# Splitting an inverse transform and its DRAM scratch into channel halves, with later weight loads and four projection steps moved into the softmax

## The chip, the cores and the metric

The kernel runs on one core of one Trainium2 chip. The metric is the device time of one execution in microseconds (us). Most executions of one kernel agree within about 1 per cent here. A profiled execution also has a "span", first instruction to last, which is 1 to 2 us shorter than the device time; times of single events below are in that span.

Engines: PE is the matmul engine, DVE the vector engine, ACT the scalar engine, POOL is GpSimd, and SP issues most DMA transfers (in a timeline "SPq" is its queue). Each engine has its own instruction list, in an order fixed before the run.

## The reference, cut to what matters

There are two independent halves, whose outputs are put side by side. S = 2048 positions, D = 576 channels, bf16.

```python
# A: attention over 8 positions, 2 apart, 32 heads of 18 channels
q, k, v = split(x @ wqkv)
logits = einsum("bhsd,bhswd->bhsw", q, kg) / sqrt(18)      # kg: k at s, s-2, ... s-14
a = einsum("bhsw,bhswd->bhsd", softmax(masked logits), vg) @ wo
# B: gated long convolution
kv = causal_conv4(k, shift_k) * v                          # four taps
y  = irfft(rfft(pad(kv)) * rfft(pad(ssm_k)))[:S] + kv * ssm_D
b  = q * y
out = concatenate([a, b], axis=-1)
```

## The kernel before

Half A and half B are interleaved so that the PE always has something to do. In time there are six stages:

1. **Front.** x is loaded, transposed on PE and evicted to SBUF as `xT`.
2. **q/k and first transform.** 18 q/k projection steps, mixed with 8 "x steps" (four-tap convolution on DVE, then a DFT matmul "s1") and 8 "k steps" (the filter, transposed on PE, then s1). Results go to DRAM scratch `Dx` and `Dk`.
3. **Products.** DVE multiplies q with shifted k, PE sums over channels to logits. Beside it: 16 v projection steps and 8 filter spectrum steps. At its end three "halo" copies bring v rows from the neighbouring partitions (`vX`).
4. **Softmax.** Nearly all DVE and ACT.
5. **Main stage.** "PV pairs" (attention weights times v on DVE, summed and projected on PE), mixed with "spectrum steps" `g_step`: load from `Dx`, second DFT stage, multiply by the filter spectrum, inverse second stage, store to `Dy`.
6. **Tail.** `y_step`: load from `Dy` in the other order, last inverse stage, times q, store.

`Dk`, `Dx` and `Dy` are scratch tensors in DRAM, through which the transform changes the order of its data. Each `Dy` load needs data of all spectrum steps. The parts that matter, cut (`...`):

```python
    load_x(0, nc.sync); load_x(1, nc.scalar); load_w(0, nc.sync); load_w(1, nc.scalar)
    load_x(2, nc.sync); load_x(3, nc.scalar)
    ...
    def s1_chunk(src, c2, Dd, vst_pool, add_d):
        for ch in range(3):
            ps = psb()                     # PSUM ring of two; q/k steps use another, psA
            ...                            # matmuls, then an ACT copy to vst
        nc.sync.dma_start(by_f1(Dd, c2), vst[:]...)
    def k_step(c2):
        ptr = pb.tile([128, 2, 1024], BF16, name="psB")
        ...                                # 10 transposes of the filter into ptr
        nc.vector.tensor_copy(kt[:], ptr[:, :, 0:D])
        s1_chunk(kt, c2, Dk, kvp, True)
    ...
    sk_step()                              # load the four taps, reorder them on DVE (skb)
    load_w(2, nc.sync)                     # v weights, into the third part of tile wq
    ...                                    # filter loads
    run(qk_steps, b_steps)                 # two lists, interleaved evenly
    permute_wv()                           # ACT: v weights into (d, h) order
    ...
    wk = pool("wk", 2, "right")
    def kh_step(g):
        Wk = wk.tile([128, 4, D], BF16, name="Wk")
        nc.sync.dma_start(Wk[:], by_rt(Dk)[:, 4 * g:4 * g + 4, :])
        ...
    def g_step(g):
        Wx = b2.tile([128, 4, D], BF16, name="Wx")
        nc.sync.dma_start(Wx[:], by_rt(Dx)[:, 4 * g:4 * g + 4, :])
        ...
    for g in range(8):
        mixed += v_steps[2 * g:2 * g + 2] + [lambda g=g: kh_step(g)]
    run([... logit_step(wi) for 8 wi], [ia_tables] + mixed + [halo])
    lg.release(); qk.release(); wk.release()
    sm = pool("sm", 2, "left")
    b2 = pool("b2", 2, "right")            # the pool of Wx exists only from here on
    softmax_a(0); softmax_a(1)
    g_step(0)
    softmax_b(0); softmax_b(1)
    run([... at_step(wp) for 4 wp], [lambda: g_step(1)])
    ...
    run([... pv_step(tp) for tp in range(4)],    [... g_step(g) for g in range(2, 8)])
    run([... pv_step(tp) for tp in range(4, 8)], [... y_step(c2) for c2 in range(8)])
```

Of the kernel before, what the change touches and what calls it, by code (L numbers as in the profile page):

```python
# [18 lines left out]
def kernel(  # L19
# [20 lines left out]
    NT = 16  # L40
    PS = bass.MemoryType.PSUM
# [17 lines left out]
    def psb():  # L59
        return pb.tile([128, 2, 512], FP32, name="psB")  # L60
# [4 lines left out]
    Dk = dram.tile([32, 128, D], BF16, name="Dk")  # L65
    Dx = dram.tile([32, 128, D], BF16, name="Dx")
    Dy = dram.tile([32, 128, D], BF16, name="Dy")
# [12 lines left out]
    def by_f1(Dd, c2):  # L80
        return Dd.rearrange("r f d -> f r d")[:, 4 * c2:4 * c2 + 4, :]

    def by_rt(Dd):
        return Dd.rearrange("r (l h) d -> (r l) h d", h=32)
# [21 lines left out]
    wq = wqp.tile([128, 5, 3 * D], BF16, name="wq")  # L106
# [26 lines left out]
    nc.gpsimd.memset(wq[0:64, 4, :], 0.0)  # L133

# [135 lines left out]
    def s1_chunk(src, c2, Dd, vst_pool, add_d):  # L270
        sf = src.rearrange("p t d -> p (t d)")
        vst = vst_pool.tile([128, 2, 2 * D], BF16, name="vst")
        for ch in range(3):
            ps = psb()
            for ri in range(2):
                extra = add_d and c2 == 0 and ri == 0 and ch < 2
                nc.tensor.matmul(ps[:, ri, 0:384], T1[:, ri, :], sf[:, 384 * ch:384 * ch + 384], start=True, stop=not extra)  # L277
                if extra:
                    n = 384 if ch == 0 else 192
                    nc.tensor.matmul(ps[:, ri, 0:n], row0[:], Db[:, 384 * ch:384 * ch + n], start=False, stop=True)  # L280
            nc.scalar.activation(vst[:, :, 384 * ch:384 * ch + 384], ps[:, :, 0:384], ACT.Copy)  # L281
        nc.sync.dma_start(by_f1(Dd, c2), vst[:].rearrange("p r (t d) -> p (r t) d", t=2))
# [12 lines left out]

    def permute_wv():
        for kb in range(5):
            nc.scalar.activation(wv[:, kb, :].rearrange("p (d h) -> p d h", h=H),
                                 wq[:, kb, 2 * D:3 * D].rearrange("p (h d) -> p d h", d=DH), ACT.Copy)
# [12 lines left out]
    def sk_step():  # L312
        skraw = kvp.tile([128, D, 4], BF16, name="tB", bufs=1)
        nc.sync.dma_start(skraw[:], B_shift_k.partition_broadcast(128))
        nc.vector.tensor_copy(skb[:], skraw[:].rearrange("p d j -> p j d"))
# [33 lines left out]
    load_w(2, nc.sync)  # L349
# [14 lines left out]
    permute_wv()  # L364
# [6 lines left out]
    Khat = kf.tile([128, 2, 32 // 2, D], BF16, name="Khat")  # L371
# [3 lines left out]
    wk = pool("wk", 2, "right")  # L375
# [63 lines left out]
    def s2(Wt, g, dst, scale):  # L439
        for prl in range(2):  # L440
            for d0, d1 in DCH:
                ps = psb()
                for im in range(2):
                    for hp in range(2):
                        nc.tensor.matmul(ps[64 * hp:64 * hp + 64, im, 0:288],  # L445
                                         W2[:, im, 4 * g + 2 * prl + hp].rearrange("p l f -> p (l f)"),
                                         Wt[:, 2 * prl + hp, d0:d1], start=True, stop=True, tile_position=(0, 64 * hp))
                nc.scalar.activation(dst[:, :, prl, d0:d1], ps[:, :, 0:288], ACT.Copy, scale=scale)  # L448
# [15 lines left out]
    def kh_step(g):  # L464
        Wk = wk.tile([128, 4, D], BF16, name="Wk")
        nc.sync.dma_start(Wk[:], by_rt(Dk)[:, 4 * g:4 * g + 4, :])
        s2(Wk, g, Khat[:, :, 2 * g:2 * g + 2, :], 1.0 / 2048)

    def g_step(g):
        Wx = b2.tile([128, 4, D], BF16, name="Wx")  # L470
        nc.sync.dma_start(Wx[:], by_rt(Dx)[:, 4 * g:4 * g + 4, :])
        Kc = Khat[:, :, 2 * g:2 * g + 2, :]
        Xc = b2.tile([128, 2, 2, D], BF16, name="Xc")
        s2(Wx, g, Xc, 1.0)
        m1 = b2.tile([128, 2, 2, D], BF16, name="m1")
        m2 = b2.tile([128, 2, 2, D], BF16, name="m2", bufs=1)
        nc.vector.tensor_tensor(m1[:], Xc[:], Kc[:, 0].unsqueeze(1).to_broadcast([128, 2, 2, D]), ALU.mult)  # L477
        nc.vector.tensor_tensor(m2[:], Xc[:], Kc[:, 1].unsqueeze(1).to_broadcast([128, 2, 2, D]), ALU.mult)  # L478
        nc.vector.tensor_tensor(m1[:, 0], m1[:, 0], m2[:, 1], ALU.subtract)
        nc.vector.tensor_tensor(m1[:, 1], m1[:, 1], m2[:, 0], ALU.add)  # L480
        Y = b2.tile([128, 4, D], BF16, name="Y")
        for prl in range(2):
            for d0, d1 in DCH:
                ps = psb()
                for zi in range(2):
                    for hp in range(2):
                        nc.tensor.matmul(ps[:, hp, 0:288], IAt[64 * hp:64 * hp + 64, zi, 2 * g + prl, :],  # L487
                                         m1[64 * hp:64 * hp + 64, zi, prl, d0:d1], start=(zi == 0), stop=(zi == 1),
                                         tile_position=(64 * hp, 0))
                nc.scalar.activation(Y[:, 2 * prl:2 * prl + 2, d0:d1], ps[:, :, 0:288], ACT.Copy)  # L490
        nc.sync.dma_start(by_rt(Dy)[:, 4 * g:4 * g + 4, :], Y[:])

    mixed = []
    for g in range(8):
        mixed += v_steps[2 * g:2 * g + 2] + [lambda g=g: kh_step(g)]
# [6 lines left out]
    run([lambda wi=wi: logit_step(wi) for wi in range(W)], [ia_tables] + mixed + [halo])  # L502
    lg.release()
    qk.release()
    wk.release()
# [4 lines left out]
    g_step(0)  # L510
    softmax_b(0)
# [46 lines left out]
    def y_step(c2):  # L558
        Vw = b2.tile([128, 4, D], BF16, name="Wx")
        Vy = Vw[:].rearrange("p (r t) d -> p r t d", r=2)  # L560
        nc.sync.dma_start(Vw[:], by_f1(Dy, c2))
        qt = b2.tile([128, 2, 2, D], BF16, name="Xc")[:, 0]
        nc.gpsimd.dma_start(qt, qb[:, 2 * c2:2 * c2 + 2, :])
        stage = b2.tile([128, 4, D], BF16, name="Y")[:, 0:2]
        for u in range(2):
            ps = psb()
            for di, (d0, d1) in enumerate(DCH):
                for ri in range(2):
                    nc.tensor.matmul(ps[:, di, 0:288], IB[:, ri, :], Vy[:, ri, u, d0:d1], start=(ri == 0), stop=(ri == 1))  # L569
            nc.vector.tensor_tensor(stage[:, u, :].rearrange("p (i d) -> p i d", i=2), ps[:, :, 0:288],  # L570
                                    qt[:, u, :].rearrange("p (i d) -> p i d", i=2), ALU.mult)
        nc.sync.dma_start(outb[:, 2 * c2:2 * c2 + 2, D:2 * D], stage)

    run([lambda tp=tp: pv_step(tp) for tp in range(4)], [lambda g=g: g_step(g) for g in range(2, 8)])
    run([lambda tp=tp: pv_step(tp) for tp in range(4, 8)], [lambda c2=c2: y_step(c2) for c2 in range(8)])
    a3.release()
    b2.release()
    kf.release()
# [30 lines left out]
```

## Time and profile before

309.3 us, median of three runs (307.89 to 309.55).

Busy time by stage of the kernel before. The stretches were chosen at the first q/k matmul, the first product, the first mask add of the softmax, the first P and the last `Dy` store. The columns: stretch, its length, then busy time and instruction count of each engine, the TensorE clock granted (1.00 is full), the share of time in which DMA engines were busy, GB/s.

```profile
core 0: us, PE busy (x) PEld busy (x) DVE busy (x) ACT busy (x) POOL busy (x), PEclk, DMA share, GB/s
0.00:29.14 29.14, 9.59 (x80) 8.52 (x81) 12.39 (x34) 12.37 (x12) 8.74 (x31) 1.00 0.96 305
29.14:100.86 71.72, 70.61 (x397) 36.24 (x396) 48.47 (x40) 51.42 (x67) 0.00 (x0) 1.00 0.53 188
100.86:150.80 49.94, 46.74 (x500) 28.63 (x500) 43.14 (x30) 35.07 (x58) 3.84 (x6) 1.00 0.43 132
150.80:176.50 25.70, 5.09 (x48) 3.92 (x48) 16.57 (x24) 11.38 (x15) 7.29 (x15) 0.67 0.56 148
176.50:264.05 87.55, 80.03 (x924) 54.13 (x924) 68.89 (x47) 51.49 (x86) 1.09 (x2) 0.94 0.32 109
264.05:308.40 44.35, 24.80 (x181) 15.96 (x180) 12.06 (x17) 4.24 (x7) 3.23 (x6) 0.68 0.70 226
```

The second and third stretch look PE-bound, 117 of 122 us. In the fourth, the softmax, the PE does 5 us of work in 26. The fifth is PE-bound again. In the last, PE, DVE and DMA take turns waiting.

The SP queue of the kernel before (start, length, line, count), from the end of the product stage. L498 is the first halo copy, L471 the loads of the spectrum steps, L491 a `Dy` store, L561 the loads of the y steps:

```profile
147.81 0.59 SPq L498 DMA_DIRECT2D vX<-vX  x1
...
151.94 21.63 SPq L471 DMA_DIRECT2D Wx<-Dx  x3
183.50 0.32 SPq L491 DMA_DIRECT2D Dy<-Y  x1
...
264.05 0.32 SPq L491 DMA_DIRECT2D Dy<-Y  x1
...
267.76 7.66 SPq L561 DMA_DIRECT2D Wx<-Dy  x3
```

And what the PE does in the softmax stage: 17 us of nothing, then transposes of attention weights (L433), then the first spectrum step (L445):

```profile
167.29 1.89 PE L433 MATMUL psA<-ident,Lsb 128*128 128x128 bf16 x16 [17.15 <-DVE Lsb L426]
...
170.75 0.68 PE L445 MATMUL psB<-Wx,W 128*64 128x288 bf16 x8
```

All eight y loads come after the last `Dy` store at 264.05.

### The profile page before, as it was taken

To read this page: it belongs to the slowest core of one execution; us is meant where nothing else is said; L and a number is where in the kernel's file an instruction comes from. 1 tells how busy PE (TensorE), PEld (TensorE's weight loads), DVE (VectorE), ACT (ScalarE), POOL (GpSimd) and SP (SyncE) were. 2 spreads that over 40 slices of the span, in tenths; PEclk is the share of its full clock that TensorE was granted. 3 is DMA by queue.
4 is the path that set the end of the run, shared out by engine and by line. 5 is a ranking of instruction groups with operands and counts; after the bars stand their busy time and mean duration, and the time that the engine had idled before them with its cause. 6 is when DMAs were issued, how large, how long until landed. Compare 5 with 4: busy or idle time off the path is not lost.

```text
span 308.4 us, 5069 instructions
## 1 busy us (share of the span) xinstructions
PE 236.9 (77%) x2129; PEld 147.4 (48%) x2129; DVE 201.5 (65%) x188; ACT 166.0 (54%) x242; POOL 24.2 (8%) x59
## 2 busy tenths in 40 slices
PE   1047999999998889999402379999989989976522
PEld 1045445555446455657102236648657657743211
DVE  3076997988501899899576496868939939323431
ACT  2165367788878457787461634765674773411000
POOL 8200000000000000000922000000000000001100
PEclk9999999999999999999955958999999999978555
DMA  7999365744545444522792213433541232359991
GB/s 238 360 364 278 149 210 175 268 153 154 212 149 179 158 155 149 155 79 76 219 231 60 78 42 113 152 119 117 191 132 64 112 121 79 133 165 368 286 301 49
DMA packets 28002, 52.37 MB, mean 170 GB/s; under 512 B 1918, under 2 KB 22094, under 8 KB 27853
## 3 DMA queue, kind: packets, MB, share of 16 engines
q1 hardware_dynamic: 25052, 47.04, 46.0%
q0 software_dynamic: 1264, 3.17, 4.0%
q10 hardware_dynamic: 1664, 1.84, 1.8%
q8 instruction: 16, 0.26, 0.4%
q14 instruction: 6, 0.05, 0.1%
HBM read 31.11 MB, written 18.87 MB: 162 GB/s over the span
## 4 chain that ended last, share of the span: by engine, by line
PE 49%; DVE 15%; DMA 14%; ACT 11%; issue 9%; SPq 0%; POOL 0%; DVEq 0%; ACTq 0%; POOLq 0%
PE psA L246 11%; PE psB L445 7%; PE psA L233 6%; PE psB L277 6%; DMA wq<-in_A_wqkv_dram 5%; DMA Xc<-in_B_q_dram 5%; PE psA L541 4%; DVE P L532 3%; PE psB L290 3%; PE psA L554 3%; PE psB L487 3%; PE psA L388 3%; ACT Y L490 3%; DMA Wx<-Dy 2%; DVE m L478 2%
## 5 line engine op out<-in xcount | busy, mean ns | idle before, releaser
L532 DVE TENSOR_TENSOR P<-vX,at 128x4608 bf16<-128x4608 bf16 x16 | 40.5, 2554 | 14.3 <-PE psA L541 14.3
L541 PE MATMUL psA<-ident,P 128*128 128x128 bf16 (+1 forms) x640 | 44.6, 223 | 5.9 <-DVE P L532 5.9
L541 PEld LDWEIGHTS <-P 128*128 128x128 bf16 (+1 forms) x640 | 38.0, 101 | 14.8 <-issue 7.6
L246 PE MATMUL psA<-xT,wq 128*128 128x512 bf16 x160 | 40.0, 384 | 0.5 <-DVE xT L149 0.5
L281 ACT ACTIVATE vst<-psB 128x768 bf16<-128x768 f32 x48 | 35.9, 814 | 4.9 <-PE psB L277 3.5
L385 DVE TENSOR_TENSOR prod<-q,k 128x4096 bf16<-128x4096 bf16 x16 | 36.0, 2287 | 2.0 <-PE psA L388 2.0
L570 DVE TENSOR_TENSOR Y<-psB,Xc 128x576 bf16<-128x576 f32 x16 | 11.6, 754 | 29.0 <-PE psB L569 16.7
L490 ACT ACTIVATE Y<-psB 128x576 bf16<-128x576 f32 x32 | 18.9, 650 | 19.1 <-PE psB L487 15.1
L554 PE MATMUL psA<-wv,xT 128*128 128x288 bf16 x160 | 25.8, 292 | 1.6 <-ACT xT L547 1.5
L569 PE MATMUL psB<-Wx,IB 128*128 128x288 bf16 x64 | 14.9, 404 | 15.3 <-DMA Wx<-Dy 15.2
L233 PE MATMUL psA<-wv,xT 128*128 128x288 bf16 x160 | 24.6, 292 | 0.2 <-ACT vX L235 0.2
L144 PE MATMUL psA<-ident,xnat 128*128 128x128 bf16 x80 | 9.6, 308 | 19.0 <-DVE xT L149 10.5
L246 PEld LDWEIGHTS <-wq 128*128 128x128 bf16 x160 | 15.4, 99 | 16.7 <-issue 1.5
L448 ACT ACTIVATE Xc<-psB 128x576 bf16<-128x576 f32 x32 | 20.1, 654 | 3.2 <-PE psB L445 2.6
L233 PEld LDWEIGHTS <-xT 128*128 128x128 bf16 x160 | 19.4, 145 | 4.7 <-issue 4.3
L448 ACT ACTIVATE Khat<-psB 128x576 bf16<-128x576 f32 x32 | 19.7, 650 | 3.5 <-PE psB L445 3.0
L554 PEld LDWEIGHTS <-xT 128*128 128x128 bf16 x160 | 13.7, 99 | 10.8 <-issue 4.5
L524 POOL DMA_DIRECT2D wv<-in_A_wo_dram x18 | 8.9, 500 | 125.6 <-PE psA L233 119.8
L569 PEld LDWEIGHTS <-IB 128*128 128x128 bf16 x64 | 7.8, 130 | 21.8 <-DMA Wx<-Dy 16.1
L293 DVE COPY kTt<-psB 128x1152 bf16<-128x1152 bf16 x8 | 6.1, 758 | 18.4 <-PE psB L290 18.3
L477 DVE TENSOR_TENSOR m<-Xc,Khat 128x2304 bf16<-128x2304 bf16 x8 | 10.8, 1356 | 10.9 <-ACT Xc L448 10.9
L144 PEld LDWEIGHTS <-xnat 128*128 128x128 bf16 x80 | 8.4, 144 | 19.9 <-issue 13.5
(116 smaller groups left out, 349.2 us busy)
## 6 DMA issues: line engine op xcount, KB each, us to landing
Dx<-vst SPq DMA_DIRECT2D x8, 576.0 KB, 3.0
Dk<-vst SPq DMA_DIRECT2D x8, 576.0 KB, 3.0
Wk<-Dk SPq DMA_DIRECT2D x8, 576.0 KB, 3.7
Wx<-Dx SPq DMA_DIRECT2D x8, 576.0 KB, 3.8
Dy<-Y SPq DMA_DIRECT2D x8, 576.0 KB, 2.7
Wx<-Dy SPq DMA_DIRECT2D x8, 576.0 KB, 5.8
kX<-in_B_k_dram SPq DMA_DIRECT2D x3, 1008.0 KB, 5.2
vt<-in_B_v_dram SPq DMA_DIRECT2D x4, 576.0 KB, 8.9
```

What stands on the lines that cost most here:

```text
L233: nc.tensor.matmul(ps[:, di, 0:288], xTt[:, kb, t2, :], wv[:, kb, d0:d1], start=(kb == 0), stop=(kb == 4))
L246: nc.tensor.matmul(ps[:, u, :], wcols(kb, comp, ct), xT[:, kb, 512 * j:512 * j + 512], start=(kb == 0), stop=(kb == 4))
L277: nc.tensor.matmul(ps[:, ri, 0:384], T1[:, ri, :], sf[:, 384 * ch:384 * ch + 384], start=True, stop=not extra)
L281: nc.scalar.activation(vst[:, :, 384 * ch:384 * ch + 384], ps[:, :, 0:384], ACT.Copy)
L385: nc.vector.tensor_tensor(prod[:], q2[ct // 2][:], k2[ct // 2][:, :, sh:sh + S], ALU.mult)
L445: nc.tensor.matmul(ps[64 * hp:64 * hp + 64, im, 0:288], W2[:, im, 4 * g + 2 * prl + hp].rearrange("p l f -> p (l f)"), Wt[:, 2 * prl + hp, ...
L448: nc.scalar.activation(dst[:, :, prl, d0:d1], ps[:, :, 0:288], ACT.Copy, scale=scale)
L490: nc.scalar.activation(Y[:, 2 * prl:2 * prl + 2, d0:d1], ps[:, :, 0:288], ACT.Copy)
L532: nc.vector.tensor_tensor(P[:].rearrange("p w (d h) -> p w d h", h=H), vs, at[:, :, t2, :].unsqueeze(2).to_broadcast([128, W, DH, H]), ALU ...
L541: nc.tensor.matmul(oacc[0:csz, ci, 128 * u:128 * u + 128], Ps[u][:, wi, 128 * ct:128 * ct + csz], ident[:], start=(ci % 2 == 0 and u == 0 ...
L554: nc.tensor.matmul(pso[:, di, 0:288], oT[:, ct, t2, :], wot[:, ct, d0:d1], start=(ct == 0), stop=(ct == 4))
L569: nc.tensor.matmul(ps[:, di, 0:288], IB[:, ri, :], Vy[:, ri, u, d0:d1], start=(ri == 0), stop=(ri == 1))
```

## The change

Its intent has three parts:

1. *Front.* Taps and v weights are loaded behind the x transposes, so that x and q/k need not share DMA and engines with them, and q/k can start earlier.
2. *v projection.* Four of the sixteen v steps move from the product stage into the softmax, and the halo copies behind them.
3. *Channel halves.* `Dk`, `Dx` and `Dy` are split into halves of 288 channels, so that y steps of the first half need only spectrum steps 0 to 3. The order of late steps is changed with it. All scratch loads share one pool of three buffers.

The diff, cut:

```diff
-    Dk = dram.tile([32, 128, D], BF16, name="Dk")          # Dx, Dy likewise
+    Dk = dram.tile([2, 32, 128, HD], BF16, name="Dk")
-    wq = wqp.tile([128, 5, 3 * D], BF16, name="wq")
+    wq = wqp.tile([128, 5, 2 * D], BF16, name="wq")
...
+    wraw = k2[1][:]...      # areas of q and k tiles, which reuse the x buffers
+    sraw = q2[1][:]...
...
     sk_step()
-    load_w(2, nc.sync)
+    load_wv()
+    permute_wv()            # ACT, 5 copies, now ahead of the q/k evictions
...
     run(qk_steps, b_steps)
-    permute_wv()
...
-    wk = pool("wk", 2, "right")
+    wk = pool("wk", 3, "right")
...
+    def load_wt(Dd, dh, g):
+        Wt = wk.tile([128, 8, HD], BF16, name="Wt")
+        nc.sync.dma_start(Wt[:], by_rt(Dd, dh, g))
+        return Wt
-    def g_step(g):
-        Wx = b2.tile([128, 4, D], BF16, name="Wx")
-        nc.sync.dma_start(Wx[:], by_rt(Dx)[:, 4 * g:4 * g + 4, :])
+    def g_step(i):
+        dh, g = i // 4, i % 4
+        Wt = load_wt(Dx, dh, g)
...
-        Y = b2.tile([128, 4, D], BF16, name="Y")
+        Y = b2.tile([128, 8, HD], BF16, name="Y", bufs=1)
...
-        mixed += v_steps[2 * g:2 * g + 2] + [lambda g=g: kh_step(g)]
+        mixed += [lambda g=g: kh_step(g)] + (v_steps[2 * g:2 * g + 2] if g < 4 else v_steps[g + 4:g + 5])
-    run([... logit_step ...], [ia_tables] + mixed + [halo])
+    run([... logit_step ...], [ia_tables] + mixed)
...
-    wk.release()
...
     g_step(0)
+    for t2 in range(12, 16):
+        v_step(t2)
+    halo()
...
-    run([... pv_step(tp) for tp in range(4)],    [... g_step(g) for g in range(2, 8)])
-    run([... pv_step(tp) for tp in range(4, 8)], [... y_step(c2) for c2 in range(8)])
+    run([... pv_step(tp) for tp in range(3)],    [... g_step(g) for g in range(2, 6)])
+    run([... pv_step(tp) for tp in range(3, 5)], [... g_step(g) for g in range(6, 8)])
+    run([... pv_step(tp) for tp in range(5, 8)], [... y_step(i) for i in range(8)])
```

## The prediction

> **What bounds it now** (busy time by stretch, 308.4 us span)
> - 0 to 29.1 us: DMA share 0.96, PE busy 9.6. The chain of waits opens with 17.9 us of weight DMA. Timeline: the taps' copy (skb) sits on DVE ahead of the xT copies and waits 10.3 us for its load; ACT waits 8.6 us for the v weights and permutes them (five times 1.25) ahead of its xT copies. So x transposes stop from 8 to 18 us; q/k matmuls start at 29.1.
> - 29.1 to 150.8: PE busy 117 of 122. In the product part (from 100.9) DVE has 41.4 us of products in 50, PE most of the 16 v steps (1.3 each).
> - 150.8 to 176.5: softmax, PE busy 5; then to 268: 84 of 91.5.
> - 268 to 308.4: PE busy 21 at clock 0.64, DMA share 0.73. The last Dy store is issued at 264.1, all eight Dy loads from 267.8 on: no inverse step can begin before the last spectral step is stored. 9.2 MB then move at about 310 GB/s.
>
> **What the change does**
> 1. Taps and v weights go into tiles that reuse the x buffers, so cannot precede the x copies. x lands by 13 us; q/k start at about 15. The first conv input still lands near 30, but PE has 39 us of independent q/k work, and DVE's conv chain (4 times 10.9, plus 6 of copies) ends near 84. The stage ends near 89 instead of 103: gain 11 to 14.
> 2. Four v steps (5.2 us of PE) go to the softmax, where PE idles; the product stage falls towards DVE's 41.4: gain 4 to 6. The halo copy (10 us to landing) starts later: neutral.
> 3. Channel halves: inverse loads of the first half need only spectral steps 0 to 3, and the last spectral step now precedes pv 5 to 7. After it remain about 30 us of PE, 27 of DVE, 22 to 28 of DMA, overlapped. PE also keeps its clock (Trainium skill, "TensorE: Matmul & The Clock Gate", Part 1: it halves after an idle window of about 3.4 us; the trace agrees: 0.50 from 283 us). Ideal gain 30, I count 18.
> 4. Cost: 576 B rows for Dk, Dx, Dy, q, output. DMA packet records show 51 ns for 1152 B and 178 for 4608, so about 30 for 576 (estimate, linear): about 6 us of DMA more in the tail, 5 in the s1 stage (share 0.53, hidden).
>
> **Critical path.** All on it: 12 + 5 + 18, about 36 of 309.3 us.
>
> **Predicted: 272 us, 80% range 258 to 289.** Faster by over 2%: 0.95, within 2%: 0.03, slower: 0.02.
>
> **Right or wrong, by step.** (1) First q/k matmul near 15 us; no skb copy before the xT copies. (2) First to last product 43 to 46 us; v matmuls in the softmax. (3) Dy loads of half 0 issued before the last Dy store; PE idle after that store below 12 us; clock near 1 until the last few us. (4) 576 B packets near 30 ns.
>
> **What would make it wrong.** The sync queue issues in order: the waits of taps and v weights may hold back the conv inputs. Half 0's Dy loads may stand behind the last Dy store, or conv work on PE ahead of ready q/k work. DVE (76% busy in the main stage) may become the limit.

## More of the kernel before

In the kernel before, a load landed at 162.15, and the matmuls that need it ran at 170.75, because others stood ahead of them in PE's list.

Where the PE starts its q/k work and its s1 work (timeline of PE; start, length, line, tiles, count, in brackets the idle time before and what ended it):

```profile
29.14 14.85 PE L246 MATMUL psA<-xT,wq 128*128 128x512 bf16 x65 [0.52 <-DVE xT L149]
43.84 0.81 PE L277 MATMUL psB<-tA,T 128*128 128x384 bf16 x4
```

The load of spectrum step 0 is issued behind the halo, at 151.94, and lands at 162.15; its matmuls stand in PE's order behind the first attention transposes, so they run only at 170.75, although the PE idled for 17 us before that.

## The result, and the profile after

The changed kernel takes 296.12 us (293.14 to 296.45, four runs) against 309.03 for the kernel before in the same rounds. The ratio is 0.9566, 95% interval 0.9497 to 0.9634. (A ratio is the mean time of one kernel's runs over that of the other's of the same rounds, so it is not quite the ratio of the medians that are quoted.) Executions over 1.5% slower than the fastest of the same kernel are left out of the means. The kernel is faster, by 13 us instead of the 36 predicted, and lies outside the predicted range of 258 to 289.

The same six stretches after the change:

```profile
0.00:21.17 21.17, 9.50 (x80) 8.38 (x81) 11.76 (x33) 7.03 (x7) 8.75 (x32) 1.00 0.93 306
21.17:107.76 86.59, 73.99 (x377) 35.25 (x376) 49.85 (x41) 56.92 (x69) 0.00 (x0) 0.90 0.59 183
107.76:156.60 48.84, 47.26 (x486) 27.22 (x488) 43.26 (x31) 32.43 (x55) 0.00 (x0) 0.97 0.51 157
156.60:190.35 33.75, 19.09 (x152) 12.70 (x149) 25.24 (x33) 23.59 (x36) 13.44 (x23) 0.71 0.68 195
190.35:260.60 70.25, 65.27 (x764) 47.91 (x764) 55.31 (x36) 40.80 (x66) 0.00 (x0) 0.92 0.32 107
260.60:294.60 34.00, 26.11 (x276) 21.15 (x273) 15.90 (x18) 6.70 (x11) 3.74 (x5) 0.93 0.80 244
```

Set against the rows of before, the first product starts 6.9 us *later* (107.76 for 100.86) although q/k start 8 us earlier. The product stage is only 1.1 us shorter. The softmax stage is 8 us longer, with 14 us more PE work in it. The main stage is 17.3 us shorter, and the tail 10.4.

**Front.** The PE of the changed kernel in the front:

```profile
21.17 10.09 PE L248 MATMUL psA<-xT,wq 128*128 128x512 bf16 x40 [0.60 <-ACT xT L149]
39.34 9.72 PE L248 MATMUL psA<-xT,wq 128*128 128x512 bf16 x33 [8.07 <-ACT q L251]
48.90 0.81 PE L279 MATMUL psB<-tA,T 128*128 128x384 bf16 x4
```

and its ACT, where L309 is the permutation of the v weights and L251 the q/k evictions:

```profile
32.29 5.95 ACT L309 ACTIVATE wv<-k 128x576 bf16<-128x576 bf16 x5 [4.15 <-DMA k<-in_A_wqkv_dram]
38.26 1.02 ACT L251 ACTIVATE q<-psA 128x1024 bf16<-128x1024 f32 x1
```

The v weights, now loaded last, land at 32.3. ACT's list has their permutation ahead of the third q/k eviction, so ACT waits 4.15 us and then permutes for 5.95; both PSUM buffers of the q/k steps stay full, and the PE stands 8.07 us.

**Softmax.** The SP queue of the changed kernel; L475 are the loads of the spectrum steps, L511 and L513 the first and third halo copy, L504 a `Dy` store, L577 the loads of the y steps:

```profile
145.33 14.07 SPq L475 DMA_DIRECT2D Wt<-Dx  x4
168.44 0.60 SPq L511 DMA_DIRECT2D vX<-vX  x1
169.52 0.33 SPq L504 DMA_DIRECT2D Dy<-Y  x1
...
171.94 2.63 SPq L513 DMA_DIRECT2D vX<-vX  x1
...
230.37 0.37 SPq L577 DMA_DIRECT2D Wt<-Dy  x1
...
260.63 0.33 SPq L504 DMA_DIRECT2D Dy<-Y  x1
```

and its ACT and DVE just before the first P (L547): ACT evicts the attention weights (L445), then step 1's `Y` (L503); DVE has the spectral products of step 2 (L491) ahead of P:

```profile
175.37 4.25 ACT L445 ACTIVATE at<-psA 128x512 bf16<-128x512 bf16 x8 [3.01 <-PE psA L443]
...
180.86 1.19 ACT L503 ACTIVATE Y<-psB 128x576 bf16<-128x576 f32 x2 [1.24 <-DMA Dy<-Y]
...
186.34 1.36 DVE L491 TENSOR_TENSOR m<-Xc,Khat 128x2304 bf16<-128x2304 bf16 x1 [8.12 <-ACT Xc L457]
...
190.35 7.49 DVE L547 TENSOR_TENSOR P<-vX,at 128x4608 bf16<-128x4608 bf16 x3
```

Two things have moved against each other. The first spectrum load is now issued at 145.33, ahead of everything, and the first `Dy` store comes at 169.52 instead of 183.50. But the halo, 147.81 before, comes at 168.44, and the first P at 190.35 instead of 176.48. The last attention weights were ready at 179.62 (end of their eviction), so P came 10.7 us after them. The last halo copy landed at 182.9, which accounts for 3.3 us. For the other 7.4 P stood in DVE's list behind the products of step 2. These waited 8.12 us for their input from ACT, whose list has step 1's `Y` eviction ahead of it; and that eviction first waited 1.24 us for the first `Dy` store to land (180.75), since the changed kernel has one `Y` buffer where the kernel before has two.

**Tail.** The first y load is issued at 230.37, 30 us ahead of the last `Dy` store, as the halves intend.

### The profile page after: what moved, and what is told of

The parts are those of the page before. It is cut to its first block, busy times and chain, and to the rows that moved or that the text cites. A ratio compares the mean times of both kernels' runs of the same rounds, so it can differ in the third digit from the quotient of the medians.

```text
span 294.6 us, 5101 instructions
## 1 busy us (share of the span) xinstructions
PE 241.2 (82%) x2129; PEld 152.6 (52%) x2129; DVE 201.3 (68%) x188; ACT 167.5 (57%) x242; POOL 25.9 (9%) x60
## 3 DMA queue, kind: packets, MB, share of 16 engines
q1 hardware_dynamic: 39644, 47.04, 50.4%
## 4 chain that ended last, share of the span: by engine, by line
PE 50%; ACT 17%; DMA 16%; DVE 11%; issue 5%; SPq 1%; DVEq 0%; ACTq 0%
PE psA L248 9%; PE psA L235 7%; PE psB L279 6%; PE psA L556 5%; PE psB L454 5%; PE psA L569 5%; DMA out_dram<-m 4%; DMA xnat<-in_A_x_dram 4%; ACT Xc L457 4%; DMA Dy<-Y 4%; DMA k<-in_A_wqkv_dram 4%; PE psB L293 3%; PE psA L398 3%; ACT Y L503 3%; ACT vst L283 3%
## 5 line engine op out<-in xcount | busy, mean ns | idle before, releaser
L248 PE MATMUL psA<-xT,wq 128*128 128x512 bf16 x160 | 42.7, 407 | 8.7 <-ACT q L251 8.1
L556 PE MATMUL psA<-ident,P 128*128 128x128 bf16 (+1 forms) x640 | 46.2, 231 | 1.5 <-DVE P L547 1.4
L556 PEld LDWEIGHTS <-P 128*128 128x128 bf16 (+1 forms) x640 | 40.9, 107 | 8.4 <-issue 4.6
L547 DVE TENSOR_TENSOR P<-vX,at 128x4608 bf16<-128x4608 bf16 x16 | 40.1, 2550 | 4.3 <-PE psA L556 4.3
L248 PEld LDWEIGHTS <-wq 128*128 128x128 bf16 x160 | 16.2, 103 | 27.8 <-issue 14.1
L454 PE MATMUL psB<-Wt,W 128*64 128x288 bf16 x256 | 28.0, 312 | 1.5 <-ACT Y L503 0.6
L560 ACT ACTIVATE xT<-psA 128x1024 bf16<-128x1024 f32 x8 | 8.2, 1024 | 34.8 <-PE psA L556 34.8
L500 PE MATMUL psB<-m,IAt 64*128 64x288 bf16 x128 | 14.9, 320 | 14.2 <-DVE m L493 7.6
L235 PE MATMUL psA<-wv,xT 128*128 128x288 bf16 x160 | 25.3, 294 | 0.3 <-ACT vX L237 0.3
L491 DVE TENSOR_TENSOR m<-Xc,Khat 128x2304 bf16<-128x2304 bf16 x8 | 10.8, 1356 | 18.6 <-ACT Xc L457 18.6
L503 ACT ACTIVATE Y<-psB 128x576 bf16<-128x576 f32 x32 | 18.9, 650 | 7.4 <-PE psB L500 6.1
L569 PE MATMUL psA<-wv,xT 128*128 128x288 bf16 x160 | 22.3, 287 | 0.0
L235 PEld LDWEIGHTS <-xT 128*128 128x128 bf16 x160 | 18.8, 147 | 6.8 <-issue 6.8
L587 DVE TENSOR_TENSOR m<-psB,Lsb 128x576 bf16<-128x576 f32 x16 | 11.4, 752 | 14.6 <-DMA out_dram<-m 8.2
L457 ACT ACTIVATE Xc<-psB 128x576 bf16<-128x576 f32 x32 | 19.6, 651 | 1.3 <-PE psB L454 1.1
L454 PEld LDWEIGHTS <-W 128*64 128x64 bf16 x256 | 12.7, 112 | 13.5 <-issue 11.9
```

Of the source, the lines that this page charges most:

```text
L235: nc.tensor.matmul(ps[:, di, 0:288], xTt[:, kb, t2, :], wv[:, kb, d0:d1], start=(kb == 0), stop=(kb == 4))
L248: nc.tensor.matmul(ps[:, u, :], wcols(kb, comp, ct), xT[:, kb, 512 * j:512 * j + 512], start=(kb == 0), stop=(kb == 4))
L454: nc.tensor.matmul(ps[64 * hp:64 * hp + 64, im, 0:HD], W2[:, im, 8 * g + 2 * prl + hp].rearrange("p l f -> p (l f)"), Wt[:, 2 * prl + hp, ...
L457: nc.scalar.activation(dst[:, :, prl, :], ps[:, :, 0:HD], ACT.Copy, scale=scale)
L500: nc.tensor.matmul(ps[:, hp, 0:HD], IAt[64 * hp:64 * hp + 64, zi, 4 * g + prl, :], m1[64 * hp:64 * hp + 64, zi, prl, :], start=(zi == 0), ...
L503: nc.scalar.activation(Y[:, 2 * prl:2 * prl + 2, :], ps[:, :, 0:HD], ACT.Copy)
```

## The experiments

Eighteen kernels ran; each was correct, and each was timed in three rounds beside the kernel before, whose median was 307.9 to 309.6 us. Medians of four runs each (the profiled one included), and intervals. The medians of front_undone_kt, loads_last and halves_only contain one slow run each, and are 290.70, 288.44 and 281.11 without it.

| run | what it is | median us | ratio to before, 95% |
|---|---|---|---|
| after | the change | 296.12 | 0.9566 [0.9497, 0.9634] |
| front_undone | change without its front part | 291.48 | 0.9435 [0.9367, 0.9502] |
| front_only | before with the front part only | 314.24 | 1.0157 [1.0113, 1.0200] |
| perm_pool | after, permutation on GpSimd | 296.35 | 0.9580 [0.9534, 0.9626] |
| perm_pool_taps | the same, taps early | 292.54 | 0.9459 [0.9414, 0.9504] |
| kt_other_psum | after, filter transposes in psA | 292.06 | 0.9442 [0.9383, 0.9500] |
| front_undone_kt | front undone and transposes in psA | 291.48 | 0.9408 [0.9349, 0.9467] |
| no_permute_taps | after, no permutation at all, taps early | 367.71 | 1.1895 [1.1826, 1.1964] |
| no_permute_taps_kt | the same, transposes in psA | 363.92 | 1.1777 [1.1693, 1.1861] |
| loads_last | after, front that blocks nobody | 288.75 | 0.9358 [0.9300, 0.9417] |
| loads_last_kt | the same, transposes in psA, q/k first | 295.07 | 0.9558 [0.9511, 0.9604] |
| v_back | change without its second part | 285.95 | 0.9278 [0.9228, 0.9329] |
| v_only | before with the second part only | 301.97 | 0.9782 [0.9733, 0.9830] |
| order_old | after, late order of before | 293.44 | 0.9506 [0.9459, 0.9554] |
| halves_only | change without first and second part | 281.50 | 0.9124 [0.9066, 0.9181] |
| early_load_only | before with the shared pool of three buffers only | 287.39 | 0.9317 [0.9261, 0.9373] |
| halves_late_load | halves_only without that pool | 298.29 | 0.9687 [0.9642, 0.9733] |
| combined | loads_last, v_back and order_old together | 278.32 | 0.9031 [0.8981, 0.9081] |
| combined_y_early | combined, half-0 y steps earlier | 283.42 | 0.9193 [0.9141, 0.9246] |

### The front part: front_undone and front_only

The theory was that the front part of the change costs time. One run takes it out of the changed kernel, the other puts it alone into the kernel before (the diff of the front above, reversed or alone).

> The changed kernel with its first part undone: taps and v weights loaded early into tiles of their own, as before; halves and moved v steps kept. Theory A (chain): the q/k and convolution stage ends when its first convolution matmul starts plus eight pairs of steps at about 7 us each, and how early q/k starts does not matter. Theory B (stall): the changed kernel lost its gain only to the 8 us for which PE waits behind the v permutation. Both say here: first q/k matmul back near 29 us, first convolution matmul near 44 (48.9 in the changed kernel), first product near 101 instead of 107.8, and the total 5 to 8 us below the changed kernel, 288 to 291.

> The kernel before with the first part of the change alone. Theory A and theory B alike: first q/k matmul near 21 us, PE waits about 8 us behind the v permutation, first product near 106 to 108 instead of 100.9, total 313 to 317, slower than before by 1 to 2.5%. If the loss in the changed kernel came from the other two parts, this one would be at or below 305.

front_undone is 4.6 us faster than the change, front_only 4.9 us slower than the kernel before (1.57 per cent of 309). Both have the same sign and nearly the same size, so the front part costs about 5 us in both surroundings. In front_only the q/k matmuls start at 20.7 and the first product at 106.1, against 29.1 and 100.9 before.

### What in the front costs: perm_pool, perm_pool_taps, kt_other_psum, front_undone_kt

Theory B blames the 8 us stall behind the permutation. perm_pool moves the permutation to GpSimd, where no eviction waits behind it (and puts the q/k steps whose tiles hold the raw weights last). perm_pool_taps also loads the taps early again, into a tile of their own.

```diff
-            nc.scalar.activation(wv[p0:128, kb, :]..., wraw[p0:128, kb, :]..., ACT.Copy)
+            nc.gpsimd.tensor_copy(wv[p0:128, kb, :]..., wraw[p0:128, kb, :]...)
```

Theory A says that from its first s1 matmul on the stage has a pace of its own, so that neither an earlier q/k start nor a filled stall shortens it. A candidate for the pacemaker is the ring of two psB buffers, through which both the filter transposes and all s1 results go. kt_other_psum moves the transposes to the other ring:

```diff
     def k_step(c2):
-        ptr = pb.tile([128, 2, 1024], BF16, name="psB")
+        ptr = pa.tile([128, 2, 1024], BF16, name="psA")
```

> The changed kernel with the PE wait taken away: the v permutation moves from ACT to the idle GpSimd, and the q/k steps that write the two borrowed tiles come last; loads and their order unchanged. Theory A (chain): no PE wait of 8 us, first convolution matmul near 44.5 us (its input is ready at 44.0), then eight pairs at 7 us: first product near 103, total 290 to 293. Theory B (stall): PE is the limit of this stage, so the 8 us and the 2 us of half clock behind it come off whole: first product at 98 or earlier, total 286 or less.

> As the run before it, and the taps are loaded ahead of the filter and k loads, into a tile of their own, while their copy on DVE still cannot precede the x copies. Theory A (chain): the first convolution operation starts when k lands, near 27 us instead of 31.8, the first convolution matmul near 39.5, first product near 98, total 285 to 289: 3 to 5 us better than the run before it. Theory B (stall): PE has q/k work anyway, so within 1 us of the run before it.

> The changed kernel with one word altered: the transposes of the filter (ten per k step) go into the PSUM pool of the q/k steps instead of the one that the convolution matmuls and their evictions share. Theory A (ring): the pairs of steps take 7 us because transposes, their DVE copy and the next first matmul (about 2 us) stand in a ring of two PSUM buffers. Then the pairs fall to 5.3 to 6 us where no q/k work is left, first product at 101 to 105 (107.8 in the changed kernel), total 290 to 294. Theory C (engine work): the 7 us are work of ACT, DVE and PE; then pairs stay at 7 us, total 295 to 298.

> The same alteration where q/k starts at 29 us (the first part undone). Theory A: PE has 72 us of work in this stage, so with the ring out of the way PE is the limit: first product near 101.5 to 102.5 (103.3 without it), total lower by 1 to 2 us only, 289.5 to 291. Theory C: no difference.

In perm_pool the stall is gone: q/k matmuls run without a pause from 21.3 to 38.7. Yet the time is that of the change, 296.35, and the first product starts at 107.1. The PE line that follows shows why:

```profile
47.69 1.44 PE L279 MATMUL psB<-tA,T 128*128 128x384 bf16 x4 [8.99 <-DVE tA L348]
```

The idle time has only moved. After about 73 of the 160 q/k matmuls of this line (L248) the first s1 is next in PE's list, and PE stands 8.99 us for its convolution input, with q/k work left behind it. So taking away this stall alone gains nothing, and theory B, that its 8 us come off whole, falls in that form. perm_pool_taps gains 3.6 us against the change, because the convolution input is ready earlier (first s1 at 44.7). kt_other_psum gains 4.1 us in the median but only 2.5 us at the first product; front_undone_kt gains over front_undone 1.0 us at the first product. The ring is a limit, but not the only one.

perm_pool showed a side effect. DVE (L342, two tensors from SBUF) and POOL (L309, the five copies) in perm_pool:

```profile
30.67 1.36 DVE L342 TENSOR_TENSOR tA<-kX,skb 128x2304 bf16<-128x2304 bf16 x1
31.94 2.38 DVE L342 TENSOR_TENSOR tB<-kX,skb 128x2304 bf16<-128x2304 bf16 x1
...
31.31 10.93 POOL L309 COPY wv<-k 128x576 bf16<-128x576 bf16 x5 [15.16 <-DMA k<-in_A_wqkv_dram]
```

While GpSimd copied, each DVE instruction on two SBUF tensors took 2.25 to 2.38 us instead of 1.36, five of them, so the convolution lost about 5 us. The Trainium skill, "SBUF — State Buffer", section "Who interferes with whom", says that a DVE instruction with two SBUF inputs contends with a GpSimd instruction that reads SBUF, and that their shared ports are an exclusive lock; five DVE instructions lengthened beside five copies, spread over the same 11 us, agree with that.

### A front without any permutation: no_permute_taps, no_permute_taps_kt

Here the v matmuls read the raw weights in place, with a step of 36 bytes between elements, so that nothing need be permuted and nothing can block.

```diff
-                nc.tensor.matmul(ps[:, di, 0:288], xTt[:, kb, t2, :], wv[:, kb, d0:d1],
+                nc.tensor.matmul(ps[:, di, 0:288].rearrange("p (d h) -> p d h", h=H), xTt[:, kb, t2, :],
+                                 wv[:, kb, :].rearrange("p (h d) -> p d h", d=DH)[:, 9 * di:9 * di + 9, :],
```

> The changed kernel without the v permutation: v weights loaded straight into their tile, and the v matmuls read them with a stride of 36 bytes; taps loaded ahead of the filter into their own tile. Nothing waits on ACT or GpSimd any more. Theory A (chain): first convolution operation near 27 us (k lands), first convolution matmul near 39.5, first product 58 us later, 97 to 99, total 285 to 289. Theory B (PE is the limit): first product at 93 to 95, total 281 to 284. If strided reads slow the v matmuls, they take over 300 ns each instead of 294.

> The run before it with the filter transposes in the other PSUM pool. Theory A (ring): now an early q/k start pays, first product at 92 to 96, total 280 to 284, below every version so far. Theory C: as the run before it.

As a whole these runs fail, 60 us slower than before, for a reason I had not foreseen. The v matmuls of the changed kernel, then of no_permute_taps, from the groups by line (busy us, mean ns, idle before):

```profile
L235 PE MATMUL psA<-wv,xT 128*128 128x288 bf16 x160 | 25.3, 294 | 0.3 <-ACT vX L237 0.3
```

```profile
L236 PE MATMUL psA<-wv,xT 128*128 128x288 bf16 x160 | 88.0, 699 | 0.0
```

The same 160 matmuls take 699 ns each instead of 294, and as they overlap in the PE, the busy time is the better measure: 88.0 us instead of 25.3. The granted clock is not the cause: 115 of them ran at a clock of 0.50 and 45 at 1.00, with medians of 698 and 697 ns. (It is odd enough that the clock fell there at all: from 103.8 to 220 us the PE shows as busy for 115.5 of 116.2, and the clock still averaged about 0.6. Why stays open.) They lie behind the front, so the front of these runs can still be read. The permutation blocks nothing there: q/k start at 20.2, the first s1 at 42.3, and the first product comes at 103.8, still 61.4 us after the first s1. With the transposes in psA it comes at 100.7, 54.4 us after.

### The same, cheaply: loads_last, loads_last_kt

Raw v weights go back into the weight tile and are loaded last, behind the filter; the permutation goes back behind the stage; the taps come first and the first convolution inputs ahead of the filter. loads_last_kt also has the transposes in psA and the first eight q/k steps ahead of the first convolution step.

```diff
     sk_step()
-    load_w(2, nc.sync)
+    kvt[0] = kv_step(0)
     ...                                    # filter loads
+    load_w(2, nc.sync)
     ...
-    run(qk_steps, b_steps)                 # loads_last_kt only
+    for st in qk_steps[:8]: st()
+    run(qk_steps[8:], b_steps[:12])
+    for st in b_steps[12:]: st()
```

(The diff is shown against the front of the kernel before; all else is the changed kernel.)

> The kernel after with a front that blocks nobody: raw v weights in the weight tile's third part as in the kernel before, but loaded last, behind the filter; taps loaded first; the first convolution chunk's inputs loaded ahead of the filter; the v weights permuted after the stage. So q/k start early as the change meant, without the permute on ACT in front and without GpSimd copies. Theory A (from the first s1 matmul on, the stage takes 56 to 61 us whatever comes before it): first q/k matmul at 19 to 22 us, first s1 at 40 to 44, first product at 98 to 102; the kernel at 287 to 291 us. Theory B (the early permute is what cost the gain, and without it the front yields the predicted 11 to 14 us): first product at 88 to 92 us, the kernel at 278 to 283 us.

> The same, with the filter transposes in the other PSUM ring, the first eight q/k steps ahead of the first convolution chunk in the program and no q/k step behind the twelfth of the sixteen convolution and filter steps. Theory A with the ring of two PSUM buffers as the pacer of the steps that have no q/k work beside them: the last steps run at under 6.4 us a pair, first product at 90 to 96 us, the kernel 279 to 287 us. Rival: the pace is set by PE and ACT work and not by the ring; then pairs stay at 6.9 to 7 us, first product at 98 to 102 us and the kernel no better than the run before this one.

loads_last takes 288.75 us (288.44 without its slow run), over 7 less than the change. Its first s1 comes at 39.3 and its first product at 98.9, where theory A expected 98 to 102 and theory B 88 to 92. One expectation was missed: q/k start at 25.8, not at 19 to 22, because the DVE copy of the taps again stands ahead of the x copies (the x transposes wait 9.7 us for them). loads_last_kt fails. Eight q/k steps ahead push the first s1 to 48.2, and at the end of the stage ACT's evictions wait for stores of the two staging buffers to land (1.41 and 1.09 us on `Dk`); the last `Dk` store is issued at 110.7, against 102.5 in loads_last. The expected pace of under 6.4 us a pair did not come. I had named one pacemaker, and taking it away uncovered another.

Across all runs of the front, the time from the first s1 matmul to the first product:

| run | first q/k | first s1 | first product | s1 to product |
|---|---|---|---|---|
| before | 29.1 | 43.8 | 100.9 | 57.0 |
| front_undone | 29.3 | 45.6 | 103.3 | 57.7 |
| front_only | 20.7 | 48.4 | 106.1 | 57.8 |
| after | 21.2 | 48.9 | 107.8 | 58.9 |
| perm_pool | 21.3 | 47.7 | 107.1 | 59.4 |
| perm_pool_taps | 20.9 | 44.7 | 105.9 | 61.2 |
| no_permute_taps | 20.2 | 42.3 | 103.8 | 61.4 |
| loads_last | 25.8 | 39.3 | 98.9 | 59.7 |
| kt_other_psum | 21.0 | 46.4 | 105.3 | 58.9 |
| front_undone_kt | 28.6 | 46.8 | 102.3 | 55.5 |
| no_permute_taps_kt | 20.5 | 46.2 | 100.7 | 54.4 |

First q/k varies by 9 us, and the first product does not follow it. It follows the first s1, if loosely (the interval between the two spreads over 7 us), which waits for the convolution on DVE and so for the taps and the first inputs. After it, eight pairs of x and k steps follow; their `Dk` stores are 7.3 us apart on average in the kernel before, 7.6 in the change and 7.9 in loads_last, and still 6.9 in the change when the q/k work is done. (loads_last_kt is left out: there the products begin before the last k steps have ended.) In the mixed part of the kernel before the PE is about 98% busy and ACT has 4.9 us of s1 and 2.3 us of q/k evictions a pair, 7.2 in all. In the part without q/k work it is the psB ring, whose removal moved the first product by 1 to 3 us in the three pairs of runs, and then the stores. Over the whole interval the PE is busy 49 to 57 us of the 54 to 61 in these runs, so PE work that was left over when the first s1 came is a rival to a pace of the chain's own. I can't split these limits further; they are nearly equal.

### The v steps: v_back and v_only

> The kernel after with all sixteen v steps back in the product stage, two ahead of each filter step, and the halo copies at the end of that stage (the second part of the change undone, nothing else). Theory: the four moved steps did not shorten the product stage by their 6 us of PE, because its pace is shared with the DVE's products, but they delayed the halo copies to 168 us and put v evictions among the exponentials. Then the product stage goes from 48.8 to about 50 to 52 us, the first P comes about 27 to 30 us after the first mask add instead of 33.8, and the kernel takes 290 to 294 us. Rival, the prediction's own step 2: the moved steps fill idle PE time for nothing, and taking them back costs 4 to 6 us: 299 to 302 us, with the product stage at 53 to 55 us.

> The kernel before with only the second part of the change: four v steps moved from the product stage into the softmax, halo copies behind them. Theory (a late halo delays the first P, whatever else is changed): product stage 49 to 50 us, first P some 5 to 10 us later after the first mask add than the 25.7 of before, kernel 313 to 319 us. Rival (the cost comes only with the single Y buffer and the halves' step order): within 2 us of before.

(Both edits also turn the order of v steps and filter steps within the product stage.)

v_back is 10.2 us faster than the change, where my own prediction's step would have it 4 to 6 slower. Its product stage takes 50.1 us instead of 48.8, so moving 5 us of PE work off it gave 1.3 us. The halo and DVE lines of v_back:

```profile
153.82 0.60 SPq L511 DMA_DIRECT2D vX<-vX  x1
...
180.95 5.03 DVE L544 TENSOR_TENSOR P<-vX,at 128x4608 bf16<-128x4608 bf16 x2 [2.91 <-ACT at L445]
```

P now starts 0.03 us after the last attention weights are there, where it came 10.7 us after them in the change. From there on the two kernels run alike (105.2 and 104.3 us to the end). The late halo and the v steps were not separated from one another.

v_only was the surprise: alone in the kernel before, the same moved steps *gain* 7 us, where I expected a loss of 4 to 10. Its SP queue:

```profile
150.19 13.03 SPq L471 DMA_DIRECT2D Wx<-Dx  x3
164.66 0.60 SPq L498 DMA_DIRECT2D vX<-vX  x1
...
171.25 0.35 SPq L491 DMA_DIRECT2D Dy<-Y  x1
```

The first P is indeed 6.9 us later than before (183.41 for 176.48), as the theory said. But with the halo gone from the end of the product stage, the first spectrum load goes ahead of it. It is issued only 1.75 us earlier, but lands in 3.65 us where it took 10.21 behind the halo (153.84 for 162.15). Spectrum step 0 runs at 155.7 instead of 170.75, its `Dy` store comes 12 us earlier (171.25 for 183.50), and the last one 4.8 us earlier. The gain is real, yet it isn't PE work taken off the product stage, whose length is 49.6 us for 50.0. It is an earlier spectrum step. In the changed kernel that was already there, so only the late P was left.

### The halves: order_old, halves_only

> The kernel after with the order of the steps of before in the last two stages (PV pairs 0 to 3 among spectrum steps 2 to 7, PV pairs 4 to 7 among the eight y steps), the channel halves kept. Theory: the halves themselves give the gain, since y loads of half 0 only need half of the stores; then within 3 us of the kernel after, 294 to 299 us. Rival: the gain of the late stages comes from moving the PV pairs against the spectrum steps, and the halves give little: 303 us or more.

> The change with its first and second part undone: only the channel halves of the inverse transform and of the DRAM scratch, with their step order. If the parts add up (front costs about 5 us, moved v steps cost about 10 us): 279 to 284 us, a gain of 26 to 30 us for the halves alone. If the prediction's 18 us for the halves is right and the parts depend on one another: 289 to 293 us. First product at about 103 us, product stage about 50 us, first P about 25 to 28 us after the first mask add.

With the late order of before, the changed kernel takes 293.44 us, within 3 us and if anything faster; the new order is not where the gain comes from. halves_only, which is the third part alone, takes 281.50 us (281.11 without its slow run), a gain of about 27 us (27.1 by the ratio) where 18 were predicted. The parts then add up: 281.5, plus the cost of the front (v_back minus halves_only, 4.5) and of the v steps (front_undone minus halves_only, 10.0), is 296.0; the change measured 296.1.

### Is it the halves, or the buffers? early_load_only, halves_late_load

v_only pointed to an earlier first spectrum load. The third part of the change also has one, hidden in a buffer change: the loads of spectrum steps take a buffer of pool `wk`, which exists in the product stage, instead of `b2`, which is made after it. Two runs separate this from the halves. (The pool also has a third buffer, which no run separates from its early existence.) early_load_only is the kernel before with the pool and nothing else:

```diff
-    wk = pool("wk", 2, "right")
+    wk = pool("wk", 3, "right")
...
-        Wx = b2.tile([128, 4, D], BF16, name="Wx")          # g_step
+        Wx = wk.tile([128, 4, D], BF16, name="Wk")
...
-    wk.release()                                            # moved to the end of the kernel
...
-        Vw = b2.tile([128, 4, D], BF16, name="Wx")          # y_step
+        Vw = wk.tile([128, 4, D], BF16, name="Wk")
```

halves_late_load makes the reverse edit in halves_only.

> The kernel before, where the loads of the spectrum steps (and of the y steps) take buffers of the pool of the filter steps, with three buffers instead of two, so that their first loads can go in the product stage, ahead of the halo; no channel halves, nothing else. Theory (the early load is a part of the gain of its own): the matmuls of spectrum step 0 at about 151 to 157 us instead of 170.7, the first Dy store at 162 to 168 us instead of 183.5, the last one at 245 to 251 us instead of 264, the kernel 291 to 297 us, a gain of 12 to 18 us. Rival (the gain comes from the halves): within 4 us of before, 305 to 310 us.

> halves_only with the loads of the spectrum and y steps back in a pool of two buffers made after the product stage, as in the kernel before. Theory: spectrum step 0 comes behind the halo again, the first Dy store at about 180 us, the last one at 258 to 264 us, the tail from the last Dy store to the end stays at 31 to 35 us because it belongs to the halves; the kernel 293 to 299 us, so that the halves alone are worth 10 to 16 us. Rival: within 4 us of halves_only, 279 to 285 us.

The SP queue and the PE of early_load_only, to be held against the same lines of the kernel before:

```profile
138.39 5.97 SPq L471 DMA_DIRECT2D Wk<-Dx  x2
147.89 0.60 SPq L498 DMA_DIRECT2D vX<-vX  x1
...
163.35 0.35 SPq L491 DMA_DIRECT2D Dy<-Y  x1
```

```profile
150.15 0.68 PE L445 MATMUL psB<-Wk,W 128*64 128x288 bf16 x8
```

The load goes 13.5 us earlier, ahead of the halo, which itself stays where it was. Spectrum step 0 then stands in PE's order ahead of the attention transposes and runs at 150.15 instead of 170.75, in time that was idle. The kernel takes 287.39 us, a gain of 20.5 us, more than the 12 to 18 expected. The softmax, main and tail stretches of early_load_only, then of halves_late_load:

```profile
150.89:174.96 24.07, 11.08 (x80) 6.51 (x80) 21.08 (x30) 16.16 (x24) 7.25 (x15) 0.57 0.66 182
174.96:242.96 68.00, 63.45 (x768) 43.80 (x768) 56.41 (x37) 43.15 (x73) 1.09 (x2) 1.00 0.31 110
242.96:286.00 43.04, 29.38 (x300) 22.53 (x297) 18.96 (x19) 7.95 (x12) 3.22 (x6) 0.90 0.74 241
```

```profile
151.50:177.30 25.80, 5.55 (x48) 4.12 (x48) 16.57 (x24) 11.48 (x15) 9.56 (x18) 0.64 0.65 178
177.30:264.05 86.75, 79.09 (x925) 53.97 (x926) 68.86 (x47) 51.52 (x86) 0.00 (x0) 0.95 0.35 118
264.05:296.10 32.05, 19.06 (x181) 14.14 (x179) 11.93 (x17) 4.23 (x7) 3.74 (x5) 0.88 0.89 267
```

These rows settle that there are two gains. With the early load alone, PE work in the softmax doubles (11.08 us for 5.09), the main stage shrinks from 87.55 to 68.00, and the tail stays long (43.04 for 44.35). PE work in the softmax grew by only 6 us. The main stretch lost 156 matmuls (924 to 768), and 119 of them are now in the tail (181 to 300), PV work in time that was idle: the earlier spectrum steps let the last `Dy` store come 21 us sooner, and PV pairs move behind it. With the halves alone, softmax and main stage are those of the kernel before, to the same last `Dy` store at 264.05, and the tail shrinks from 44.35 to 32.05. ("Halves" means the halves with the change's late order; the order alone was tried only beside the early load, in order_old.) So the four corners are:

| | late load | early load |
|---|---|---|
| whole channels | 309 (before) | 287.39, ratio 0.9317 |
| channel halves | 298.29, ratio 0.9687 | 281.50, ratio 0.9124 |

By the ratios, times 309: the halves alone are worth 9.7 us, the early load alone 21.1, both 27.1. They overlap by 3.7 us.

### A version that beats both: combined, combined_y_early

combined puts together what the runs showed to be good: halves with the shared pool, the front of loads_last, all v steps and the early halo in the product stage, and the late order of before. combined_y_early places the half-0 y steps among the last spectrum steps:

```diff
-    run([... pv_step(tp) for tp in range(4)],    [... g_step(g) for g in range(2, 8)])
-    run([... pv_step(tp) for tp in range(4, 8)], [... y_step(i) for i in range(8)])
+    run([... pv_step(tp) for tp in range(2)],    [... g_step(g) for g in range(2, 6)])
+    run([... pv_step(tp) for tp in range(2, 5)], [g6, y0, y1, g7, y2, y3])
+    run([... pv_step(tp) for tp in range(5, 8)], [... y_step(i) for i in range(4, 8)])
```

> Channel halves, loads_last's front, all v steps in the product stage with the early halo, and the late order of before (PV pairs 0 to 3 among spectrum steps 2 to 7). If the single gains add up against the kernel after (loads_last 7 us, v_back 10 us, order_old 3 us): 275 to 279 us. If they overlap: 280 to 286 us.

> As combined, but the half-0 y steps stand among the last spectrum steps and PV pairs, and the last stage has three PV pairs and four y steps. Theory (the y steps of half 0 wait in PE's order behind the last spectrum steps although their data landed long before): the last Dy store comes later, but the tail from it to the end shrinks from 34 to 20 to 26 us, the kernel 271 to 277 us, some 3 us better than combined. Rival (the last stage is bound by PE work and output stores that only move): within 2 us of combined.

combined takes 278.32 us (277.63 to 280.32), 10 per cent less than the kernel before and 18 us less than the change. It is 3 us better than halves_only, which is a small difference. combined_y_early is 5 us slower: its last `Dy` store comes at 245.6 instead of 241.4, and the tail, 35.2 us, did not shrink, where 20 to 26 were expected. I had taken early data for a reason to work earlier. The tail is not short of y work that could have been done before; what paces it stays open.

## Why the prediction was wrong, point by point

- **Direction.** Faster by over 2 per cent, given 0.95, came true. The time, 272 against 296, did not.
- **Step 1, the front: predicted +12 us, measured about −5.** q/k did start earlier, at 21.2 and not at 15. The failed step is "The stage ends near 89 instead of 103", and not only its premise that q/k start at about 15. It rested on "29.1 to 150.8: PE busy 117 of 122" and on "PE has 39 us of independent q/k work", read as: PE work that starts earlier ends earlier. The runs show that PE's list puts only part of that work ahead of the first s1. In the change 74 matmuls ran between the first q/k and the first s1, in 27.7 us; in the kernel before 66 did, in 14.7. With the stall gone (perm_pool), PE ran out of them at 38.7 and stood 8.99 us. The first product then comes 54 to 61 us after the first s1 in all eleven runs of the table; why just that long stays open. In the change the first s1 came 5 us later, because its taps were loaded late and its place in PE's order is behind the stalled q/k steps. The prediction named both risks in its last paragraph ("may hold back the conv inputs", "conv work on PE ahead of ready q/k work", which is what perm_pool shows; in the change it is the other way round), but gave them no weight.
- **Step 2, the v steps: predicted +4 to +6, measured about −10 in this kernel** (v_back), and +7 alone in the kernel before (v_only), by another mechanism. The failed step is "the halo copy (10 us to landing) starts later: neutral". It starts 20 us later, lands at 182.9, and the first P comes 10.7 us after the attention weights: 3.3 us of that is the halo, 7.4 the spectral products that stand ahead of P. The landing time was about right (10.0 to 12.7 us); what waits for it was not asked. "The product stage falls towards DVE's 41.4" failed too: it fell by 1.1 us.
- **Step 3, the channel halves: predicted +18, measured about +27, with the wrong mechanism for most of it.** What the step names, y loads that need only half of the stores, is worth 9.7 us alone and lies in the tail, 44.35 to 32.05. The other 17 us of the 27 come in with the shared pool of three buffers (which is worth 21 without the halves), and the prediction does not mention it. A check of the sum alone (main stage −17.3, tail −10.4, softmax +8.1, together 19.6 against 18) would have passed this step as right. That agreement would have been luck. Only the two crossed runs showed that the step was wrong.
- **The clock** in the tail rose from 0.68 to 0.93, as predicted. The Trainium skill, "TensorE: Matmul & The Clock Gate", Part 1, has the clock at half after an idle window of about 3.4 us; the trace agrees in the front too, where the clock was 0.50 from about 34 to 44 us, in and after the 8.07 us stall. (In no_permute_taps it was halved without such a gap, see there.)
- **Step 4, the 576-byte packets: right.** The packet records of the trace of after show a median of 29.0 ns for 28,672 packets; the estimate was about 30. The share of the main queue rose from 46.0% to 50.4% of the span.

So 36 us predicted became 13: 27 from step 3, less 10 and less 5.

## What to carry to other kernels

Ask of every idle stretch what work could stand in it, and then what keeps that work out. Here PE stood idle for 17 us in the softmax. Taking a load's buffer from a pool that already exists, with a third buffer, put 6 us of work into that stage and brought all later spectrum steps forward; at 20.5 us that was worth more than the whole restructuring with its 13. When you move a step, follow the step's *last consumer*: the v steps were free to move, but the halo behind them fed the next stage, and what was placed ahead of its consumer came late too. And when one part of a change touches both data layout and buffers, cross the two in a two-by-two of runs before you credit either, because a sum that comes out right can hide two errors.

## What the Trainium skill lacked or had wrong

- "SBUF — State Buffer", in the note on cachelines of the section "Door 1: The DMA port swizzle", says that accesses which leave a 16-byte line at every element pay a penalty, but gives no figure for a matmul operand. Here 160 matmuls whose moving operand was read with a step of 36 bytes took 699 ns each instead of 294 for 288 columns, and 88.0 us of busy time instead of 25.3, a factor of 3.5.
- "SBUF — State Buffer", "Who interferes with whom", has the rule for DVE against GpSimd but no times for these two instructions. The numbers: 2.25 to 2.38 us instead of 1.36 for a 128x2304 bf16 instruction on two SBUF tensors, beside copies of 128x576 on GpSimd of 2.19 us each. Nothing in the runs contradicts the page.
- "DMA: Bandwidth & Descriptors", table "Specifications", gives 512 bytes as the least transfer for line rate. Packets of 576 bytes took 29.0 ns, of 1152 bytes 51, and of 4608 bytes 178, so 19.9, 22.6 and 25.9 bytes per ns: above 512 bytes, the larger packets still moved 30 per cent more per ns. The sizes belong to different transfers, so size is not shown to be the only cause; and the same page's section "Why small descriptors are slow (HBM only)" does count a fixed overhead per packet.
- No page that I read says that the pool from which a load's buffer is taken can decide where the load, and the work that needs it, stand in the engines' order. Here that, with a third buffer, was 20.5 us.
